# Layer 2 of batches 0 and 1 as seven quarter products, in a fused cross attention and maxout kernel

## The chip, the cores and the metric

The kernel runs on one core of one Trainium2 chip, alone. A core has five engines that run side by side and meet through semaphores: TensorE (PE; its weight loads are listed as PEld), VectorE (DVE), ScalarE (ACT), GpSimd (POOL) and SyncE (SP), which here issues nearly all DMAs. The metric is the device time of one execution in microseconds (us), the median of several runs; less is better.

## The reference

There are 8 batches, 8 heads, 512 tokens and 32 state rows of 64 columns per head. Each batch has a cross attention in both directions, and all of its 544 rows then go through a layer with two weight matrices of which the larger product is kept:

```python
scores = scale * np.matmul(x, state.transpose(0, 1, 3, 2))     # a = softmax(scores)
xread = np.matmul(a, state)
scores2 = scale * np.matmul(state, x.transpose(0, 1, 3, 2))    # a2 = softmax(scores2)
sread = np.matmul(a2, x)
x = np.concatenate([xread, sread], axis=2)                     # as rows of 8 * 64 = 512 columns
g = np.maximum(x @ w1, x @ w2)                                 # 512 -> 1024
out = g @ w_out                                                # 1024 -> 512
```

## The kernel before, in words

The larger of two products is written as relu(x (w1 - w2)) + x w2. So the kernel computes wd = w1 - w2 and wwo = w2 w_out once, and the output is relu(x wd) w_out + x wwo. For the token rows, x is A S (attention weights times state), so S is multiplied with wd and wwo first: for each batch that gives the small matrix `sw` (two groups of four heads, 1024 columns for wd and 512 for wwo, `sw_mm`, three pieces called 0, 1 and w). Layer 1 is then `l1_mm`: for each of 8 blocks f of 128 hidden columns two matmuls of `sw` with A^T (`at`), 512 columns wide, into one bank of PSUM; `relu` empties it into `r` (bf16). Layer 2 is r w_out plus A times the wwo part of `sw`; this last part is called the opening here.

Layer 2 comes in two forms. The plain one (`l2_mm`) computes for each of four chunks of 128 tokens eight matmuls with `r` and two with `at`, all 512 columns wide: 40 per batch. The other treats tokens, hidden columns and output columns each in halves, and so `r` and w_out each as 2 x 2 quarters: with sums of quarters made beforehand, seven products of quarters do for the eight of the plain form (`product`, eight matmuls of 256 columns each: four hidden blocks by two token chunks). The sums of w_out's quarters are `wt` (`w_sum` 0 to 3, once), those of r's quarters are `st` (`r_sum` 0 to 3, per batch). The products pile up in three banks called X, Y and Z: X takes products 1, 6, 7 and 4 one after the other, and between them its contents are copied to `part` (`keep`) or, with a part added, to a quarter of the output (`put`); Y takes 5 and 3, Z takes 2. `opened` adds the opening (four matmuls of 256 columns), for one quarter with the difference of two halves of `sw` (`difference`, on POOL). Before the change batches 0 and 1 use the plain form, batches 2 to 7 the other.

Where no loop says otherwise, the order is what is written. Up to the end of batch 1 the order of all engines comes from a table of tokens, ORDER: each token is a step with its batch, its part, its engine (>A is ACT, >V DVE, >P POOL) and its banks (@). It starts weights, batches 0 and 1, and the attention of batch 2. From batch 2 on a loop takes over: layer 1 of batch b, then its seven products, with scores, exponentials, `sw` and the transposes of batch b + 1 between them. A^T and X^T are made by transposing DMAs on SP's queue (`at_dma`, `xt_dma`), X^T from bf16 copies that POOL casts (`cast_b`); `cast_e` makes another copy for the state read (`sr_mm`, the attention's other direction). Every engine takes its instructions strictly in the order written, so one that waits holds up all behind it.

The state reads of batches 0 and 1 are picked out of a larger product: `srw_mm` computes more than is needed, `srw_ev` copies it to `srx`, and `sr_pick` takes four blocks per batch from it, on POOL. The ring of banks for short-lived results is `RELEASE`.

In the listings bank_63 is bank 0, bank_64 bank 1 and so on; r_105 is `r` of even batches, r_106 of odd ones; sw_102, sw_103 and sw_104 are `sw` of batches 0, 1 and 2; big_112 holds `wt`, big_114 `st`, big_115 `part` and `dif`, big_109 and big_111 the outputs of batches 0 and 1, big_117 x of batch 2, big_118 x of batch 3.

Of the kernel before, what the change touches and what calls it, by code (L numbers as in the profile page):

```python
# [8 lines left out]
F32 = mybir.dt.float32  # L9
# [33 lines left out]
mul.2.0>P l2.1.1.1@0 le.1.3>A sc.2.1@1 l2.1.1.2@0 ce.3.0>P exp.2.1>A l2.1.0.1@7 ce.3.1>P l2.0.2.3@2 red.2.1>V
l2.1.2.1@5 cb.3.0>P l2.0.3.0@3 le.1.2>V l2.0.0.3@6 mul.2.1>P l2.1.1.0@0 l2.0.0.2@6 l2.1.1.o@0 ce.3.3>P atd.2
l2.1.0.3@7 ce.3.2>P le.1.1>A l2.0.3.2@3 le.1.0>V l2.0.0.0@6 cb.3.1>P le.0.3>A sr.2@0 le.0.0>V sw.2.0@3,7 xtd.3
ldx.5.0 ldx.5.1
sw.2.w@5,1 sre.2>V swe.2.0.0>A sw.2.1@6,4 l2.0.2.0@2 swe.2.w.1>A swe.2.w.0>V l2.0.1.3@0 swe.2.1.1>A l2.0.2.1@2
swe.2.0.1>V l2.0.1.o@0 le.0.2>A l2.0.1.2@0 swe.2.1.0>A l2.0.1.0@0 srt.2@2 l2.0.1.1@0 srte.2>A le.0.1>V store.0
"""

LATE = 2

WHOLE = ()

RELEASE = [3, 1, 5, 4, 7, 6, 2, 0]


@with_exitstack
def kernel(
# [9 lines left out]
    nc = tc.nc  # L69
# [31 lines left out]
    def copy(eng, o, i):  # L101
        if eng == "A":
            nc.scalar.copy(o, i)  # L103
        elif eng == "V":
            nc.vector.tensor_copy(o, i)  # L105
        else:
            nc.gpsimd.tensor_copy(o, i)  # L107
# [168 lines left out]
    def red(b, hh):  # L276
        nc.vector.tensor_reduce(es_all[:, b, hh], e_view(e_s[b % 2], hh), axis=AXX, op=ALU.add)  # L277
        nc.vector.reciprocal(er_s[b % 2][:, hh], es_all[:, b, hh])  # L278
# [104 lines left out]
    def l2_open(b, c, p, start, stop, lo=0, hi=DM):  # L383
        for g in range(2):
            nc.tensor.matmul(p[:, lo:hi], at_s[b % 3][:, g, c, :], sw_s[b % 3][:, g, FF + lo:FF + hi],  # L385
                             start=(start and g == 0), stop=(stop and g == 1))

    def l2_f(b, c, p, fs, start, stop, lo=0, hi=DM):
        for j, f in enumerate(fs):
            nc.tensor.matmul(p[:, lo:hi], r_s[b % 2][:, f, c * 128:(c + 1) * 128], wo[:, f, lo:hi],  # L390
                             start=(start and j == 0), stop=(stop and j == len(fs) - 1))
# [16 lines left out]
    def rq(b, i, j):  # L408
        return r_s[b % 2][:, 4 * j:4 * j + 4, 256 * i:256 * i + 256]
# [57 lines left out]
    def store(b, c0=0, c1=NC, lo=0, hi=DM, eng=None):  # L467
        dst = out[b * L:b * L + S].rearrange("(p c) n -> p c n", c=NC)
        (eng or nc.sync).dma_start(out=dst[:, c0:c1, lo:hi], in_=ob(b)[:, c0:c1, lo:hi])
# [110 lines left out]
    def l2_mm(b, c, q, ring):  # L580
        p, first, last = acc(f"l2{b}{c}", ring)
        if q == "o":
            l2_open(b, c, p, first, last)
        else:
            l2_f(b, c, p, (2 * q, 2 * q + 1), first, last)

    def sw_range(b, z):
        if z == "w":
# [254 lines left out]
```

## Time and profile before

| | |
|---|---|
| median of 3 runs | 147.07 us (146.77 to 147.42) |
| the profiled execution | 147.19 us, of which the span of its instructions 145.4 us |
| granted TensorE clock, mean | 0.989 |
| TensorE busy | 136.4 us, 94% of the span |
| VectorE, ScalarE, GpSimd busy | 98.3, 82.1 and 67.9 us |
| HBM traffic | 15.20 MB read, 8.91 MB written |

A line of the groups gives the kernel's line, engine and operation, output and inputs, how often, the busy time with the mean of one, and the idle time before with what ended it. A line of the timeline gives start, length, engine, line, operation and count; a line of the chain of waits gives start, length, engine and line. "SPq" is SP's queue of DMA issues; the time that a transfer takes to land is listed apart.

### The profile page before, as it was taken

What the parts mean: (1) busy time and instruction counts of PE and PEld (TensorE: products, weight loads), DVE (VectorE), ACT (ScalarE), POOL (GpSimd) and SP (SyncE); (2) the same over time, 40 slices, a digit from 0 to 9 for tenths busy, and PEclk for the clock granted to TensorE, in tenths of its full rate; (3) what the DMA queues carried; (4) which work ended last, traced back from release to release, by engine and by line L of the source; (5) the groups of instructions that cost most, each with busy time, mean ns of one, the idle gap of its engine ahead of it and who ended that gap; (6) DMA issues with size and microseconds to landing.
All of it is one profiled execution on the core that took longest, in us unless ns stands there. A gap on an engine that the chain in (4) does not pass through costs nothing.

```text
span 145.4 us, 3491 instructions
## 1 busy us (share of the span) xinstructions
PE 136.4 (94%) x1376; PEld 89.0 (61%) x1388; DVE 98.3 (68%) x181; ACT 82.1 (56%) x157; POOL 67.9 (47%) x95
## 2 busy tenths in 40 slices
PE   6888999999999999999999999999999999999950
PEld 2566735444454446785778478757867784885840
DVE  3488969783324648997899789489948896941300
ACT  4457789898122675845781768268556817831110
POOL 4147320198979990498079509923930630000000
PEclk9999999999999999999999999999999999999995
DMA  3999999939991599999976991487316034202451
GB/s 126 331 364 394 384 387 385 327 58 174 243 359 59 97 251 393 369 136 275 384 123 138 347 285 33 72 288 149 67 42 252 7 72 185 113 0 72 155 181 38
DMA packets 36468, 29.50 MB, mean 203 GB/s; under 512 B 22624, under 2 KB 32352, under 8 KB 35552
## 3 DMA queue, kind: packets, MB, share of 16 engines
q1 hardware_dynamic: 36176, 29.10, 68.9%
q8 instruction: 12, 0.20, 0.6%
q10 hardware_dynamic: 272, 0.13, 0.3%
q14 instruction: 8, 0.07, 0.2%
HBM read 15.20 MB, written 8.91 MB: 166 GB/s over the span
## 4 chain that ended last, share of the span: by engine, by line
PE 83%; DMA 11%; ACT 1%; issue 1%; DVE 1%; SPq 0%; DVEq 0%
PE bank L427 26%; PE bank L376 19%; PE bank L390 9%; DMA big<-in_moe_w_out_dram 8%; PE bank L433 7%; PE bank L353 4%; DMA big<-in_x_dram 3%; PE bank L578 3%; PE bank L474 2%; PE bank L484 2%; PE bank L385 2%; PE bank L265 2%; PE bank L305 1%; PE bank L482 1%; ACT wo L103 1%
## 5 line engine op out<-in xcount | busy, mean ns | idle before, releaser
L371 DVE TENSOR_SCALAR r<-bank 128x512 bf16<-128x512 f32 x32 | 21.8, 691 | 13.0 <-PE bank L376 12.6
L281 POOL TENSOR_TENSOR a<-e,er 128x512 bf16<-128x512 bf16 x14 | 16.6, 1195 | 29.5 <-ACT e L273 22.5
L376 PE MATMUL bank<-at,sw 128*128 128x512 bf16 x122 | 29.4, 379 | 0.5 <-DVE sw L105 0.2
L103 ACT COPY big<-bank 128x512 f32<-128x512 f32 (+1 forms) x29 | 16.9, 587 | 17.5 <-PE bank L427 6.6
L103 ACT CAST sw<-bank 128x512 bf16<-128x512 f32 x35 | 19.5, 606 | 4.0 <-PE bank L353 4.0
L427 PEld LDWEIGHTS <-big 128*128 128x128 bf16 x192 | 17.9, 98 | 5.1 <-DVE er L278 2.1
L369 ACT ACTIVATE r<-bank 128x512 bf16<-128x512 f32 x32 | 18.5, 597 | 4.5 <-PE bank L376 4.2
L376 PEld LDWEIGHTS <-sw 128*128 128x128 bf16 x128 | 12.3, 98 | 14.1 <-ACT sw L103 0.5
L107 POOL CAST xe<-big 128x512 bf16<-128x512 f32 x27 | 17.7, 688 | 6.2 <-DMA big<-in_x_dram 6.2
L427 PE MATMUL bank<-big,big 128*128 128x256 bf16 x144 | 17.1, 273 | 0.0
L107 POOL CAST xb<-big 128x1024 bf16<-128x1024 f32 x12 | 12.2, 1040 | 7.2 <-DMA big<-in_x_dram 7.2
L390 PE MATMUL bank<-wo,r 128*128 128x512 bf16 x61 | 15.2, 379 | 0.3 <-issue 0.2
L427 PEld LDWEIGHTS <-r 128*128 128x128 bf16 x144 | 13.7, 98 | 2.6
L403 DVE TENSOR_TENSOR big<-bank,big 128x512 f32<-128x512 f32 (+1 forms) x19 | 12.3, 654 | 2.9 <-PE bank L433 2.9
L277 DVE TENSOR_REDUCE sums<-e 128x16 f32<-128x512 bf16 x16 | 10.6, 664 | 5.1 <-ACT e L273 5.0
L103 ACT COPY sread_t<-bank 128x128 bf16<-128x128 bf16 x8 | 3.3, 473 | 16.9 <-PE bank L337 13.7
L273 ACT ACTIVATE e<-bank 128x512 bf16<-128x512 f32 x16 | 9.0, 601 | 5.8 <-PE bank L265 5.7
L427 PE MATMUL bank<-wo,r 128*128 128x256 bf16 x96 | 12.3, 273 | 0.0
L433 PE MATMUL bank<-sw,at 128*128 128x256 bf16 x72 | 10.8, 273 | 0.0
L390 PEld LDWEIGHTS <-r 128*128 128x128 bf16 x64 | 5.9, 98 | 7.0 <-issue 0.5
L433 PEld LDWEIGHTS <-at 128*128 128x128 bf16 x96 | 9.4, 98 | 1.1
L403 DVE TENSOR_TENSOR big<-r 128x1024 bf16<-128x1024 bf16 x12 | 9.2, 767 | 0.6
(86 smaller groups left out, 195.9 us busy)
## 6 DMA issues: line engine op xcount, KB each, us to landing
big<-in_x_dram SPq DMA_DIRECT2D x16, 512.0 KB, 5.5
out_dram<-big SPq DMA_DIRECT2D x7, 1024.0 KB, 5.4
big<-in_moe_w_dram SPq DMA_DIRECT2D x8, 512.0 KB, 11.7
big<-in_moe_w_out_dram SPq DMA_DIRECT2D x4, 512.0 KB, 11.7
out_dram<-big SPq DMA_DIRECT2D x4, 256.0 KB, 3.5
sf<-in_state_dram SPq DMA_DIRECT2D x1, 384.0 KB, 10.4
out_dram<-w2m SPq DMA_DIRECT2D x1, 256.0 KB, 2.5
out_dram<-w2m SPq DMA_DIRECT2D x2, 128.0 KB, 3.1
```

What stands on the lines that cost most here:

```text
L103: nc.scalar.copy(o, i)
L107: nc.gpsimd.tensor_copy(o, i)
L273: nc.scalar.activation(out=e_view(e_s[b % 2], hh).rearrange("p (g c) i n -> p g c (i n)", g=2), in_=p.rearrange("p (c g m) -> p g c m", c= ...
L277: nc.vector.tensor_reduce(es_all[:, b, hh], e_view(e_s[b % 2], hh), axis=AXX, op=ALU.add)
L281: (nc.gpsimd if eng == "P" else nc.vector).tensor_mul(e_view(a_s[b % 2], hh), e_view(e_s[b % 2], hh), er_s[b % 2][:, hh].unsqueeze(3).to_b ...
L369: nc.scalar.activation(out=o, in_=p, func=ACTF.Relu)
L371: nc.vector.tensor_scalar(o, p, scalar1=0.0, scalar2=None, op0=ALU.max)
L376: nc.tensor.matmul(p, sw_s[b % 3][:, g, f * 128:(f + 1) * 128], at_s[b % 3][:, g].rearrange("p c t -> p (c t)"), start=(g == 0), stop=(g = ...
L390: nc.tensor.matmul(p[:, lo:hi], r_s[b % 2][:, f, c * 128:(c + 1) * 128], wo[:, f, lo:hi], start=(start and j == 0), stop=(stop and j == le ...
L403: (nc.gpsimd if eng == "P" else nc.vector).tensor_tensor(o, i0, i1, op=op)
L427: nc.tensor.matmul(pv[c], lhs[:, f, 128 * c:128 * c + 128], rhs[:, f, :], start=first and f == 0 and (c == 0 or pv.split), stop=False, ski ...
L433: nc.tensor.matmul(pv[c], at_s[b % 3][:, g, 2 * i + c, :], rhs[:, g, :], start=False, stop=False, skip_group_check=True)
```

## The change

Batches 0 and 1 use the seven products too. The tokens of the plain form go from the end of the table, and tokens for sums, products, copies and additions come in (p1 to p7, o3, o4, o7 and p2o for the openings, k0 to k2 for `keep`, v00 to v11 for `put`, rs for `r_sum`, dif). Besides:

- `srx` lies in the input buffer of batch 1 and not in the buffer of batch 2's small matrix, and the picks stand on POOL ahead of batch 2's casts.
- Four casts of batch 2 (ce.2) move from POOL to ACT; the weight sums 2 and 3 move from POOL to DVE.
- The store of batch 0 is issued ahead of X^T of batch 3; that of batch 1 in the loop, behind A^T of batch 3.
- `RELEASE` names the banks in another order.
- The last copy of the state rows' output is one on ACT and not two halves on DVE and ACT; in the branch for out-of-range sums, which isn't taken, a store is split.

```diff
-swe.0.w.0>V l2.1.3.2@4 ce.2.1>P l1.0.3@3 l1.0.1@1 re.1.2>A ce.2.2>P l1.1.0@6 re.0.3>A re.0.1>V l2.0.2.2@2 l1.0.6@7
...
+p1.0@1 k0.0>A p1.1@4 rs.0.2>V wt.2>V v00.0 p6.0 rs.0.3>V k0.1>A k1.0>A p5.0@7 wt.3>V v00.1 rs.1.0>V k2.0>A
+sc.2.0@6 exp.2.0>A sc.2.1@0 exp.2.1>A sw.2.0@5,3 red.2.0>V mul.2.0>P red.2.1>V swe.2.0.0>A swe.2.0.1>A ce.2.0>A ce.2.1>A ce.2.2>A ce.2.3>A
+p7.0 o7.0 v11.0 rs.1.1>V mul.2.1>P p3.0 o3.0 rs.1.2>V atd.2 sw.2.w@6,2 swe.2.w.0>A v01.0 swe.2.w.1>A
+p4.0 o4.0 rs.1.3>V ce.3.0>P ce.3.1>P cb.3.0>P ce.3.2>P ce.3.3>P cb.3.1>P v10.0>A store.0 xtd.3 dif.1>P
+sr.2@0 p6.1 k1.1>A sw.2.1@5,3 sre.2>V swe.2.1.0>A swe.2.1.1>V p5.1@7 k2.1>A
+p7.1 o7.1 v11.1 p3.1 o3.1 v01.1 srt.2@0 srte.2>A p4.1 o4.1 v10.1>A ldx.5.0 ldx.5.1
...
-RELEASE = [3, 1, 5, 4, 7, 6, 2, 0]
+RELEASE = [1, 6, 2, 5, 3, 0, 4, 7]
...
-    srx = sw_s[2].rearrange("p g w -> p (g w)")[:, 0:2080].bitcast(F32).rearrange("p (b g k z) -> p b g k z", b=2, g=2, k=4)
+    srx = big[7][:, 0:1040].rearrange("p (b g k z) -> p b g k z", b=2, g=2, k=4)
...
+    def fresh(kind, b, lhs, rhs, at):
+        pairs[kind, b] = Pair(at)
+        product(pairs[kind, b], lhs, rhs, True)
...
+        p1=lambda b, at: fresh("X", b, rq(b, 0, 0), wq(0, 0), at), p2=lambda b, at: fresh("Z", b, rq(b, 0, 1), wq(1, 0), at),
+        p5=lambda b, at: fresh("Y", b, st[:, 0], wt[:, 0], at), p6=lambda b: product(pairs["X", b], st[:, 1], wt[:, 1]),
+        p7=lambda b: product(pairs["X", b], st[:, 2], wt[:, 2]), p3=lambda b: product(pairs["Y", b], st[:, 3], wq(1, 1)),
+        p4=lambda b: product(pairs["X", b], rq(b, 1, 1), wt[:, 3]),
...
+        k0=lambda b, e: keep(0, pairs["X", b], e), k1=lambda b, e: keep(1, pairs["X", b], e),
+        k2=lambda b, e: keep(2, pairs["Y", b], e), v00=lambda b: put(b, 0, 0, pairs["Z", b], 0),
+        v11=lambda b: put(b, 1, 1, pairs["X", b], 2), v01=lambda b: put(b, 0, 1, pairs["Y", b], 1),
+        v10=lambda b, e: put(b, 1, 0, pairs["X", b], None, e),
...
-    store(1)
...
-    w_sum(3, "P")
...
+        if b == 2:
+            store(1)
...
-    m2(1, "VA", "r", 256, 512)
+    m2(1, "A", "r", 256, 512)
```

Three places show what stands where now. On DVE, from the last evacuation of layer 1 of the first two batches (L371 before, L370 now) through the two reductions of batch 2, before:

```order
L371 TENSOR_SCALAR r_106<-bank_64 128x512
L277 TENSOR_REDUCE sums_79<-e_91 128x16
L278 RECIPROCAL er_95<-sums_79 128x16
L277 TENSOR_REDUCE sums_79<-e_91 128x16
L278 RECIPROCAL er_95<-sums_79 128x16
L105 COPY big_111<-bank_68 128x512
L105 COPY big_111<-bank_70 128x512
```

and now, from the third sum of batch 0's r on:

```order
L402 TENSOR_TENSOR big_114<-r_105 128x1024
L402 TENSOR_TENSOR big_112<-wo_77 128x1024
L402 TENSOR_TENSOR big_109<-bank_66,big_115 128x2x256
L402 TENSOR_TENSOR big_114<-r_105,big_114 128x1024
L402 TENSOR_TENSOR big_112<-wo_77,big_112 128x1024
L402 TENSOR_TENSOR big_111<-bank_65,big_115 128x2x256
L402 TENSOR_TENSOR big_114<-r_106 128x1024
L276 TENSOR_REDUCE sums_79<-e_91 128x16
L277 RECIPROCAL er_95<-sums_79 128x16
L276 TENSOR_REDUCE sums_79<-e_91 128x16
L277 RECIPROCAL er_95<-sums_79 128x16
L402 TENSOR_TENSOR big_109<-bank_64,big_115 128x2x256
```

Before, nothing stood between the evacuations and the reductions, and plain copies of output chunks followed. Now sums, weight sums and additions stand ahead of the reductions, and the last row, which empties X of batch 0 (bank_64) into quarter (1,1), stands behind them.

On POOL, from the casts of batch 2 (big_117) to the attention weights of batch 2 (a_93), before:

```order
L107 CAST xb_89<-big_117 128x4x4x64
L107 CAST xe_86<-big_117 128x2x4x64 x3
L107 COPY wz_73<-sw_104 32x130 x8
L403 TENSOR_TENSOR big_112<-wo_77 128x1024 x2
L403 TENSOR_TENSOR big_112<-wo_77,big_112 128x1024
L281 TENSOR_TENSOR a_93<-e_91,er_95 128x8x64
```

and now:

```order
L402 TENSOR_TENSOR big_112<-wo_77 128x1024
L106 CAST xb_89<-big_117 128x4x4x64
L402 TENSOR_TENSOR big_112<-wo_77,big_112 128x1024
L402 TENSOR_TENSOR big_115<-sw_102 128x512
L280 TENSOR_TENSOR a_93<-e_91,er_95 128x8x64 x2
```

The eight picks (L107 COPY) stand ahead of these rows now; a weight sum has come between the two casts that X^T of batch 2 is made from, and the four casts to xe_86 are gone to ACT.

On SP, from A^T of batch 2 (at_101) to A^T of batch 3 (at_99) and what follows it, before:

```order
L286 DMA_TRANSPOSE at_101<-a_93 128x8x128
L243 DMA_TRANSPOSE xt_88<-xb_90 128x16x128
L168 DMA big_113<-in_x_dram 128x4x256 x2
L469 DMA out_dram<-big_109 128x2048
L469 DMA out_dram<-big_111 128x2048
L243 DMA_TRANSPOSE xt_87<-xb_89 128x16x128
L286 DMA_TRANSPOSE at_99<-a_94 128x8x128
L168 DMA big_117<-in_x_dram 128x4x256 x2
```

and now:

```order
L285 DMA_TRANSPOSE at_101<-a_93 128x8x128
L468 DMA out_dram<-big_109 128x2048
L242 DMA_TRANSPOSE xt_88<-xb_90 128x16x128
L167 DMA big_113<-in_x_dram 128x4x256 x2
L242 DMA_TRANSPOSE xt_87<-xb_89 128x16x128
L285 DMA_TRANSPOSE at_99<-a_94 128x8x128
L468 DMA out_dram<-big_111 128x2048
L167 DMA big_117<-in_x_dram 128x4x256 x2
```

The store of batch 0 (big_109) stands ahead of X^T of batch 3 (xt_88); that of batch 1 (big_111) has moved past X^T of batch 4 and A^T of batch 3, to just ahead of the loads of batch 6.

More of the change, by code (lines that the diff above doesn't have):

```diff
@@ L33 @@
 ww.1.3@7 sub.2.1>V ate.1.0>A ww.0.3@1 swre.1.1>A sw.1.1@0,6 sw.0.1@5,3 swe.1.1.0>A swe.1.1.1>V ww.2.3@4 swe.0.1.0>A
-swe.0.1.1>V l1.1.5@6 cw2.1>P l1.1.7@0 cw2.0>A re.1.5>V l1.0.7@3 w2.1@5 re.1.7>V re.0.7>A w2.0@6 w2e.1>V cwo.0>A
+swe.0.1.1>V l1.1.5@6 cw2.1>P srp.0>P srp.1>P l1.1.7@0 cw2.0>A re.1.5>V l1.0.7@3 w2.1@5 re.1.7>V re.0.7>A w2.0@6 w2e.1>V cwo.0>A
 l1.0.5@3 l1.1.6@0 w2e.0>V l1.1.4@5 cwo.1>A ww.2.0@4 re.0.5>V ww.1.0@7 re.1.4>A ww.2.1@4 sub.0.0>V ww.1.1@7 re.1.6>A
 sub.0.1>V ww.3.0@2 wwe.2>A ww.0.1@1 sub.1.1>V ww.3.1@2 wwe.1>A ww.0.0@1 sub.1.0>V wwe.3>A l1.0.4@7 wwe.0>A cb.2.0>P
-sw.0.0@2,4 re.0.4>V sw.1.0@0,5 swe.0.0.1>A sw.0.w@1,3 swe.1.0.1>V sw.1.w@7,6 ce.2.0>P swe.1.0.0>A l2.1.3.3@4
@@ L43 @@
[L43 to L48, printed above, removed]
+sw.0.0@2,4 re.0.4>V wt.0>P sw.1.0@0,5 swe.0.0.0>A swe.0.0.1>V sw.0.w@1,3 sw.1.w@7,6 cb.2.1>P swe.1.0.0>A swe.1.0.1>V xtd.2 wt.1>P
@@ new lines @@
+p2.1@2 l1.0.6@4 swe.0.w.0>A re.0.6>V l1.0.3@0 l1.0.2@5 swe.0.w.1>A re.0.3>V swe.1.w.0>V mS.1>A
+l1.0.1@4 l1.0.0@1 p2.0@3 swe.1.w.1>V mS.0>A Sd dif.0>P re.0.2>V re.0.1>A re.0.0>A p2o.0
+l1.1.0@7 l1.1.1@6 l1.1.2@0 l1.1.3@5 re.1.0>V re.1.1>A re.1.2>A rs.0.0>V rs.0.1>V re.1.3>A
+p2o.1 ldx.4.1 ldx.3.0 ldx.4.0 ldx.3.1
+p1.0@1 k0.0>A p1.1@4 rs.0.2>V wt.2>V v00.0 p6.0 rs.0.3>V k0.1>A k1.0>A p5.0@7 wt.3>V v00.1 rs.1.0>V k2.0>A
+sc.2.0@6 exp.2.0>A sc.2.1@0 exp.2.1>A sw.2.0@5,3 red.2.0>V mul.2.0>P red.2.1>V swe.2.0.0>A swe.2.0.1>A ce.2.0>A ce.2.1>A ce.2.2>A ce.2.3>A
@@ L563 @@
         left[f"ww{i}"] = 4
-    for b in range(2):
-        for c in range(NC):
-            left[f"l2{b}{c}"] = 5
     def acc(key, ring):
@@ L578, in ww_mm @@
             nc.tensor.matmul(p, w2t[:, f, i, :], wo[:, f, :], start=(first and f % 2 == 0), stop=(last and f % 2 == 1))
[L580 to L585, printed above, removed]
+    pairs = {}
+    def fresh(kind, b, lhs, rhs, at):
+        pairs[kind, b] = Pair(at)
+        product(pairs[kind, b], lhs, rhs, True)
     def sw_range(b, z):
@@ L601 @@
         idle=idle, fill=lambda k, r: idle(1, r, 512 if k >= 100 else 256, k >= 200), cS=s_cast, mS=lambda z, e: s_mask(z, LATE, B, e), Sd=lambda: s_dma(LATE, B), ce=cast_e, cb=cast_b, xtd=xt_dma,
-        atd=at_dma, red=lambda b, h, e: red(b, h), mul=mul, cw2=w2_cast, sub=w_sub, cwo=wo_cast, ww=ww_mm, l2=l2_mm,
-        wwe=lambda i, e: copy(e, wwo[:, i, :], open_[f"ww{i}"]), le=lambda b, c, e: l2_out(b, c, open_[f"l2{b}{c}"], e),
-        wt=w_sum,
+        atd=at_dma, red=lambda b, h, e: red(b, h), mul=mul, cw2=w2_cast, sub=w_sub, cwo=wo_cast, ww=ww_mm,
+        wwe=lambda i, e: copy(e, wwo[:, i, :], open_[f"ww{i}"]),
+        wt=w_sum, rs=r_sum, dif=difference,
+        p1=lambda b, at: fresh("X", b, rq(b, 0, 0), wq(0, 0), at), p2=lambda b, at: fresh("Z", b, rq(b, 0, 1), wq(1, 0), at),
+        p5=lambda b, at: fresh("Y", b, st[:, 0], wt[:, 0], at), p6=lambda b: product(pairs["X", b], st[:, 1], wt[:, 1]),
+        p7=lambda b: product(pairs["X", b], st[:, 2], wt[:, 2]), p3=lambda b: product(pairs["Y", b], st[:, 3], wq(1, 1)),
+        p4=lambda b: product(pairs["X", b], rq(b, 1, 1), wt[:, 3]),
+        p2o=lambda b: opened(b, pairs["Z", b], 0, so_half(b, 0)), o7=lambda b: opened(b, pairs["X", b], 1, so_half(b, 1)),
+        o3=lambda b: opened(b, pairs["Y", b], 0, so_half(b, 1)), o4=lambda b: opened(b, pairs["X", b], 1, dif[:, b % 2]),
+        k0=lambda b, e: keep(0, pairs["X", b], e), k1=lambda b, e: keep(1, pairs["X", b], e),
+        k2=lambda b, e: keep(2, pairs["Y", b], e), v00=lambda b: put(b, 0, 0, pairs["Z", b], 0),
+        v11=lambda b: put(b, 1, 1, pairs["X", b], 2), v01=lambda b: put(b, 0, 1, pairs["Y", b], 1),
+        v10=lambda b, e: put(b, 1, 0, pairs["X", b], None, e),
         Se=lambda lo, hi, j, e: s_ev(done[f"S.{lo}.{hi}"], lo, hi, j, e), store=store,
@@ L811 @@
             m2(t, "V")
-            m_store(t, nc.gpsimd)
+            for k in range(2):
+                m_store(t, nc.gpsimd, 256 * k, 256 * k + 256)
 _INS = ['x', 'state', 'moe_w1', 'moe_w2', 'moe_w_out']
```

4 lines of the change are left out of this document (removed).

## The prediction, on record before the changed kernel ran

> **What bounds the kernel now.** I read the page's busy shares first, then the chain of waits in order of time, then the busy time by stage.
>
> ```profile
> span 145.4 us, 3491 instructions
> PE 136.4 (94%) x1376; PEld 89.0 (61%) x1388; DVE 98.3 (68%) x181; ACT 82.1 (56%) x157; POOL 67.9 (47%) x95
> ...
> 29.95 0.41 PE bank L353 x8
> 43.88 3.45 PE bank L390 x16
> 52.95 0.06 PE bank L337
> 53.44 3.45 PE bank L376 x16
> 56.89 0.87 PE bank L427 x8
> 57.76 0.47 PE bank L265 x16
> 59.10 0.44 PE bank L433 x4
> 59.54 0.77 PE bank L353 x24
> 63.52 0.36 PE bank L305 x32
> ...
> 30.36:53.44 23.08, 22.82 (x169) 10.71 (x173) 10.28 (x20) 11.70 (x21) 21.60 (x27) 1.00 0.71 171
> ```
>
> The first rows are the page's; the chain's give start, length and work; the stage rows give the stretch, its length, and the busy time of PE, PEld, DVE, ACT and POOL, then the granted clock. From 29 us to the tail the chain is TensorE alone. The stage that the change rewrites runs from 30.36 (the last small matrix of batches 0 and 1, 29.95 + 0.41) to 53.44 (layer 1 of batch 2): TensorE is busy 22.82 of 23.08 us at full clock, DVE only 10.28. So TensorE work taken out there is time won, as long as DVE and ACT, which get more work, don't become what TensorE waits for; and what is won at 53.44 lasts only if the inputs of the later batches, which TensorE uses up without gaps, come earlier too.
>
> **TensorE's work.** Before, layer 2 of batches 0 and 1 is 80 matmuls of 512 columns; sixteen take 3.45 us (0.216 each): 17.25 us. Now it is 14 products of eight matmuls of 256 columns at 0.87 and 8 openings of four at 0.44: 15.70. The saving is 1.55 us, the most that this stage can give beside its 0.26 us of gaps.
>
> The Trainium skill has a rule that speaks against this (TensorE: Matmul & The Clock Gate, Back-to-back issue gap): it gives a sustained 131 ns for 512 columns and 81 for 128, which taken at its word makes 144 narrow matmuls (at least 11.7 us, an estimate from that page) dearer than 80 wide ones (10.5): 1.2 us lost. The trace disagrees: 216 ns for 512 columns and 109 for 256, just what the same section calls the isolated gap.
>
> **What DVE and ACT must now do in that stage.** Rows for the durations (start, length, engine):
>
> ```profile
> 29.58 2.05 ACT L103 CAST sw<-bank 128x512 bf16<-128x512 f32 x4 [0.16 <-PE bank L353]
> 29.89 2.48 DVE L105 CAST sw<-bank 128x512 bf16<-128x512 f32 x4
> 31.55 0.94 ACT L223 ACTIVATE sb<-sf,mask 128x768 bf16<-128x768 f32 x1
> 53.27 3.62 PE L376 MATMUL bank<-at,sw 128*128 128x512 bf16 x16
> 53.90 0.60 ACT L369 ACTIVATE r<-bank 128x512 bf16<-128x512 f32 x1 [0.41 <-PE bank L376]
> 57.72 0.69 DVE L403 TENSOR_TENSOR big<-r 128x1024 bf16<-128x1024 bf16 x1
> 58.45 0.69 DVE L403 TENSOR_TENSOR big<-big,r 128x1024 bf16<-128x1024 bf16 x1
> 59.06 0.68 DVE L277 TENSOR_REDUCE sums<-e 128x16 f32<-128x512 bf16 x1
> 60.17 2.51 POOL L281 TENSOR_TENSOR a<-e,er 128x512 bf16<-128x512 bf16 x2 [5.65 <-DVE er L278]
> 60.77 1.00 DVE L403 TENSOR_TENSOR big<-r 128x1024 bf16<-128x1024 bf16 x1
> 63.70 0.68 DVE L403 TENSOR_TENSOR big<-bank,big 128x512 f32<-128x512 f32 x1
> L103 ACT CAST xe<-big 128x512 bf16<-128x512 f32 x3 | 1.9, 618 | 3.5 <-DMA big<-in_x_dram 3.4
> ```
>
> A sum over 1024 columns takes DVE 0.69 us alone (one start to the next 0.73 as at 57.72, where it uses the one before; else I take 0.61 to 0.65, near the four casts in 2.48) and 1.00 beside POOL's products (60.17). An addition from a bank takes 0.68; two reductions with reciprocals run from 59.06 to 60.77, 1.71. An evacuation starts 0.20 us after its two matmuls (53.27 + 0.43, then 53.90). I now walk the new order from 30.36.
>
> TensorE: product 2 of batch 1 (0.87), five first-layer matmul pairs of batch 0 (0.43 each, with 0.1 of waiting for a bank), product 2 of batch 0 and its opening (1.31) end at 34.8. Batch 1's last four pairs follow; DVE evacuates the first of them from 35.4 to 36.05 and then has an unbroken queue: sums 0, 1, 2 of batch 0 (0.73 + 0.73 + 0.61), weight sum 2 (0.65), an addition (0.68), sum 3 (0.65), weight sum 3 (0.69), an addition (0.68), sum 0 of batch 1 (0.65), two reductions of batch 2 (1.71), and only then the addition that empties X of batch 0 into quarter (1,1), 0.68: done at **44.5**.
>
> TensorE meanwhile: the four pairs end at 36.53, the opening at 36.97, product 1 of both batches at 38.71, products 6 and 5 of batch 0 (after 0.05 for ACT's copy of X) at 40.5, scores 0.47, the small matrix 0.26 (a third of L353's 0.77), product 7 and opening 1.31, product 3 and opening 1.31, small matrix 0.26: **44.1**. Product 4 adds on to X, so it waits for DVE until 44.6: 0.5 us lost. Behind it on TensorE stands all else, state read of batch 2 first.
>
> ACT: four casts, two masked copies of the state (0.94 each) and five evacuations of layer 1 end at 37.6, just ahead of its first copy of X; the copies of banks (0.59) and two exponentials end at 42.5; two evacuations (0.52 each) and the four casts of batch 2 that POOL had (0.62 each) end at 46.0. Product 4 ends at 45.9 with its opening; the state read needs those casts: 0.2 lost. Then state read 0.36, product 6 of batch 1 0.87, small matrix 0.26, product 5 0.87: 48.46. ACT's copy of X of batch 1, behind two evacuations and quarter (1,0) of batch 0, ends at 48.3, so no wait. Three products with openings (3.93) and the transpose 0.06 bring layer 1 of batch 2 to **52.45** instead of 53.44: **-0.99 us**, that is, 1.55 of work and most of 0.26 of gaps less some 0.8 of new waits. Bounds: none of these waits, and layer 1 starts at 51.65 (-1.8); or DVE's seven sums before 44.5 all at 1.00, 2.2 us later (+1.2). I take my walk, because POOL has nothing between its difference for batch 0 and the products of batch 2:
>
> ```profile
> 28.67 1.04 POOL L107 CAST xb<-big 128x1024 bf16<-128x1024 f32 x1 [7.19 <-DMA big<-in_x_dram]
> 32.89 2.62 POOL L107 COPY wz<-sw 32x130 f32<-32x130 f32 x8
> 35.59 4.20 POOL L403 TENSOR_TENSOR big<-wo 128x1024 bf16<-128x1024 bf16 x2
> 43.95 1.17 POOL L107 CAST xe<-big 128x512 bf16<-128x512 f32 x2
> 31.30 2.06 SPq L243 DMA_TRANSPOSE xt<-xb  x1
> 49.23 1.80 SPq L243 DMA_TRANSPOSE xt<-xb  x1
> 54.23 0.84 SPq L469 DMA_DIRECT2D out_dram<-big  x2
> 55.17 7.74 SPq L243 DMA_TRANSPOSE xt<-xb  x1
> 63.02 1.86 SPq L286 DMA_TRANSPOSE at<-a  x1
> DMA to landing us min/median/max: 4.3/4.3/4.3
> DMA to landing us min/median/max: 10.6/10.6/10.6
> DMA to landing us min/median/max: 5.9/6.1/6.3
> sbd<-sb SPq DMA_TRANSPOSE x1, 3.7
> ```
>
> **The moved pieces.** The eight picks (2.62 us) go to POOL's idle 7.19 us before 28.67: free, and what they read is batch 1's dead input buffer. POOL from 28.67: cast 1.04, weight sum 2.1, cast 1.04, weight sum 2.1, difference some 1.2: 36.2. So X^T of batch 2 is issued at 32.9, not 31.3, and lands 4.3 later at 37.2 (the first landing row is that of 31.30 and of 49.23, the second that of 55.17, the third that of the two at 82 and 95 us). The state's transpose goes 2.06 after it and takes 3.7: 38.7. Scores read both at 40.5: hidden. At 43.0 POOL multiplies, and then has batch 3's casts without a break: 45.1 + four at 0.59 + two at 1.04, 49.6 to 50. X^T of batch 3 is thus issued about 0.6 late, and behind batch 0's store, which now goes out at 47.8 instead of 54.23. Alone it landed in 4.3 us; behind two stores and two loads (55.17) in 10.6. Here one store has a start of 2 us: I take 54 to 55 (the later ones, straight behind one store, land in 5.9 and 6.3). Its reader starts at 52.45 + 3.45 + 0.87 = 56.8: hidden with about 2 us. Batch 1's store moves behind the A^T issue of 63.02 and in front of two loads that are cast some 14 us later: nothing on the path.
>
> **The tail.**
>
> ```profile
> 139.00 0.37 ACT L103 COPY w2m<-bank 128x256 f32<-128x256 f32 x1 [0.88 <-PE bank L484]
> 140.31 0.29 DVE L105 COPY w2m<-bank 128x128 f32<-128x128 f32 x1 [3.24 <-PE bank L484]
> 140.63 0.27 ACT L103 COPY w2m<-bank 128x128 f32<-128x128 f32 x1 [1.26 <-DVE w2m L105]
> ```
>
> The two half copies ran one after the other to 140.90; one of 0.37 from 140.31 ends at 140.68: -0.22 us, ahead of the last store.
>
> Sum: 147.19 (the profiled execution: 145.4 of span and 1.8 around it, which I leave) - 0.99 - 0.22 = 145.98. The median of the runs is 0.12 below that execution: **145.9 us**.
>
> **Rivals.**
> - *All of the work is saved* (DVE's queue is done by 44.1 and ACT's casts too): 0.7 less, 145.2. For it: DVE's starts lie as close as 0.60; against it: both waits stand on full queues.
> - *DVE is the new bound.* Its 10.28 busy us grow by ten sums and six additions less the copies out, to some 18.5 of 21.5. If its seven sums before X's addition run at 1.00 as at 60.77, product 4 waits until 46.8 and all behind it is 2.2 us late: 148.2, slower. It decides from 1.2 us of extra lateness on. Against it: POOL is idle there.
> - *X^T of batch 3 is late.* Landing in 10.6 us puts the scores at 60.4, 3.6 late: 149.6. Against it: half the traffic ahead.
> - *Narrow matmuls cost more than half of wide ones.* A matmul of 256 columns that takes 0.120 instead of 0.109 eats all 1.55: 147.5 with my waits and the tail. Against it: the 0.87 rows, in every batch from 2 on. The skill's sustained figures above would end here, on the slow side.
>
> **How the numbers follow.** My walk 0.50 (own range 145.4 to 146.6), all saved 0.15, DVE the bound in whole or part 0.24, X^T late 0.08, narrow matmuls or anything else that voids the change 0.03. About 0.5% (0.74 us) is what a measurement of this kernel can tell from no change, so faster means below 146.33. Of the walk 0.42 lies below that, all of the second, and 0.04 of the third (a lateness under 0.4): 0.61. Slower, above 147.8: 0.08 of the third, 0.05 of the fourth: 0.13. The rest is 0.26. The range 145.0 to 147.4 leaves out only the full DVE case and the late X^T.
>
> **What would show it.** In the trace of the changed kernel: 144 matmuls of 256 columns between 30 and 53 us at 0.87 for eight; layer 1 of batch 2 at 52.45 (51.7 if all is saved, 54.6 if DVE binds); one TensorE wait of about 0.5 us ahead of product 4 of batch 0, released by a DVE addition; DVE without gaps from 36 to 48; X^T of batch 3 landed by 55; one 0.37 us copy at the end. I am wrong if TensorE waits over 1.5 us in that stage, or if a wait in the pass of batch 2 takes back what was won.

## The result, and the profile after

The changed kernel takes **145.74 us** (median of 9 runs, 145.60 to 146.72), the kernel before beside it 147.30 us (9 runs, 146.77 to 147.61). The ratio is 0.9908, with a 95% interval of 0.9887 to 0.9929: 1.35 us less, or 1.56 by the medians. The profiled execution took 145.66 us, its span 143.9.

The page of the changed kernel, its first rows and busy shares:

```profile
span 143.9 us, 3646 instructions
PE 136.0 (95%) x1441; PEld 95.2 (66%) x1452; DVE 106.8 (74%) x191; ACT 86.3 (60%) x166; POOL 65.3 (45%) x91
```

TensorE is busy 0.4 us less than before and not 1.55; VectorE has 8.5 us more. (A second profiled execution of the changed kernel has 135.3 us for TensorE, so this row by itself decides little.) The busy time by stretch (stretch, length, busy time of PE, PEld, DVE, ACT and POOL with their instructions, granted clock, DMA share, GB/s) shows the rewritten stage and the two passes behind it:

```profile
30.30:52.64 22.34, 22.22 (x235) 16.78 (x237) 19.29 (x32) 15.35 (x29) 15.33 (x15) 1.00 0.81 203
52.64:66.08 13.44, 13.39 (x162) 9.51 (x162) 11.74 (x22) 8.00 (x16) 9.03 (x11) 1.00 0.80 205
66.08:79.58 13.50, 13.43 (x162) 9.48 (x162) 11.93 (x23) 8.44 (x18) 8.28 (x10) 1.00 1.08 266
```

The stage took 23.08 us before and takes 22.34: 0.74 us of the 1.55 are won, and TensorE has nearly no gaps (0.12 us). The chain of waits of the changed kernel (start, length, engine and line) shows what became of the rest:

```profile
30.30 0.98 PE bank L426 x8
...
38.80 1.91 PE bank L426 x16
...
41.17 0.34 PE bank L352 x8
41.51 0.98 PE bank L426 x8
...
42.93 0.87 PE bank L426 x8
...
44.24 0.34 PE bank L352 x8
44.58 0.98 PE bank L426 x8
...
46.35 0.98 PE bank L426 x8
47.34 0.34 PE bank L352 x8
```

A product (L426, eight matmuls) takes 0.87 us, but 0.98 when it stands right behind a run of small tiles (the small matrix L352, the state read L304). And a third of the small matrix takes 0.34 by itself, where all three thirds in one place take 0.77, 0.26 each. The weight loads, some matmuls and two rows of ScalarE and VectorE of the changed kernel's timeline (start, length, line, what is loaded, and the idle time before with what ended it) show where the 0.11 comes from:

```profile
37.83 0.68 DVE L402 TENSOR_TENSOR big<-wo 128x1024 bf16<-128x1024 bf16 x1
37.95 0.59 ACT L102 COPY big<-bank 128x512 f32<-128x512 f32 x1 [0.65 <-PE bank L426]
38.77 1.66 PEld L426 LDWEIGHTS <-big 128*128 128x128 bf16 x16 [0.32 <-DVE big L402]
...
41.10 0.11 PEld L352 LDWEIGHTS <-sbd 64*32 64x32 bf16 x8
41.44 0.77 PEld L426 LDWEIGHTS <-big 128*128 128x128 bf16 x8 [0.23 <-issue]
...
42.66 0.86 PEld L426 LDWEIGHTS <-big 128*128 128x128 bf16 x8
42.76 1.04 PE L426 MATMUL bank<-wo,big 128*128 128x256 bf16 x8
...
44.51 1.05 PE L426 MATMUL bank<-big,r 128*128 128x256 bf16 x8
44.51 0.77 PEld L426 LDWEIGHTS <-r 128*128 128x128 bf16 x8 [0.23 <-issue]
```

Between products of full tiles, the first weights are loaded 0.10 us ahead of the first matmul (42.66 and 42.76). Behind the 64x32 tiles the load waits, and starts with the matmuls (44.51 both). The Trainium skill (TensorE: Matmul & The Clock Gate, "Step-by-step: what each phase is for") says that TensorE takes a weight load ahead of running matmuls where their row groups don't conflict, or into the spare weight buffer; these rows agree as far as the 0.10 goes, and why a load is not taken ahead behind small tiles no run here shows.

By work alone (14 products at 0.87, 8 openings at 0.44, 9 pairs of layer 1 at 0.43, scores 0.47, three thirds at 0.257, state read 0.36, transpose 0.06) the stage is some 21.25 us. The other 1.1 are: five products behind small tiles, 0.11 each; 0.22 for products 6 and 5 of batch 0 at 38.80, whose first weights wait (row 38.77 above), the one wait for another engine in the stage; three lone thirds, 0.25 together; small gaps in layer 1, 0.08. The profile puts that wait down to VectorE, of which a sum of quarters of w_out (row 37.83) ended at 38.51. But that sum is for product 7, and the two that product 6 reads had ended by 34.85 and 37.31. What product 6 must wait for is ScalarE's copy of X, onto which it adds: row 37.95, done at 38.54. The two ends lie 0.03 apart, so the trace does not separate them; the kernel's text speaks for ScalarE. Before, the same stage lost only 0.27 in such ways. It had the three thirds in one place, as its chain shows:

```profile
49.42 0.83 PE bank L353 x24
50.25 0.16 issue
```

SP's queue in the changed kernel's timeline (start, length of the issue, line, kind): L468 are stores, L242 X^T, L167 loads of X, L285 A^T.

```profile
50.65 2.99 SPq L242 DMA_TRANSPOSE xt<-xb  x1
...
63.92 0.52 SPq L468 DMA_DIRECT2D out_dram<-big  x1
...
67.71 7.64 SPq L242 DMA_TRANSPOSE xt<-xb  x1
75.44 2.04 SPq L285 DMA_TRANSPOSE at<-a  x1
```

The issue of X^T of batch 5 (67.71) stands on the queue for 7.64 us, with batch 1's store, two loads and batch 2's store ahead of it. Next in the queue is A^T of batch 4, which lands 4.1 us after 75.44, at 79.54; its reader starts at 79.58. So there is a second bound beside TensorE, and it touches it here.

The passes behind take what they took before to 0.03 us, except that of batch 4, which starts at this landing: 13.43 us instead of 13.30. TensorE ends at 139.60 (before: 140.29), the last copy at 139.99 (before: 140.90), and from there to the span's end it is 3.9 us (before: 4.5).

### The profile page after: what moved, and what is told of

The parts are those of the page before. It is cut to its first block, busy times and chain, and to the rows that moved or that the text cites. A ratio compares the mean times of both kernels' runs of the same rounds, so it can differ in the third digit from the quotient of the medians.

```text
span 143.9 us, 3646 instructions
## 1 busy us (share of the span) xinstructions
PE 136.0 (95%) x1441; PEld 95.2 (66%) x1452; DVE 106.8 (74%) x191; ACT 86.3 (60%) x166; POOL 65.3 (45%) x91
## 4 chain that ended last, share of the span: by engine, by line
PE 86%; DMA 6%; SPq 2%; ACT 1%; issue 1%; DVE 0%; DVEq 0%
PE bank L426 36%; PE bank L375 19%; PE bank L432 10%; DMA big<-in_moe_w_dram 6%; PE bank L352 5%; PE bank L574 4%; PE bank L473 2%; PE bank L483 2%; PE bank L264 2%; PE bank L304 2%; PE bank L516 1%; SPq L167 1%; PE bank L481 1%; PE bank L291 1%; ACT wb L102 1%
## 5 line engine op out<-in xcount | busy, mean ns | idle before, releaser
L370 DVE TENSOR_SCALAR r<-bank 128x512 bf16<-128x512 f32 x32 | 21.9, 690 | 11.9 <-PE bank L375 10.8
L102 ACT COPY big<-bank 128x512 f32<-128x512 f32 (+2 forms) x37 | 20.8, 566 | 16.1 <-PE bank L426 8.4
L426 PEld LDWEIGHTS <-big 128*128 128x128 bf16 x256 | 23.9, 98 | 6.5 <-DVE er L277 2.1
L426 PE MATMUL bank<-big,big 128*128 128x256 bf16 x192 | 23.1, 273 | 0.1
L426 PEld LDWEIGHTS <-r 128*128 128x128 bf16 x192 | 18.2, 98 | 3.7 <-issue 0.5
L402 DVE TENSOR_TENSOR big<-bank,big 128x512 f32<-128x512 f32 (+1 forms) x25 | 16.4, 660 | 3.8 <-PE bank L432 3.7
L426 PE MATMUL bank<-wo,r 128*128 128x256 bf16 x128 | 16.3, 273 | 0.0
L432 PE MATMUL bank<-sw,at 128*128 128x256 bf16 x96 | 14.4, 273 | 0.0
L432 PEld LDWEIGHTS <-at 128*128 128x128 bf16 x128 | 12.5, 98 | 1.7
L402 DVE TENSOR_TENSOR big<-r 128x1024 bf16<-128x1024 bf16 x16 | 12.6, 790 | 0.6
L402 POOL TENSOR_TENSOR big<-sw 128x512 bf16<-128x512 bf16 x8 | 9.2, 1154 | 0.9 <-POOL a L280 0.9
L426 PE MATMUL bank<-wo,big 128*128 128x256 bf16 x64 | 8.3, 273 | 0.0
```

The lines of the kernel that those rows point to most:

```text
L370: nc.vector.tensor_scalar(o, p, scalar1=0.0, scalar2=None, op0=ALU.max)
L402: (nc.gpsimd if eng == "P" else nc.vector).tensor_tensor(o, i0, i1, op=op)
L426: nc.tensor.matmul(pv[c], lhs[:, f, 128 * c:128 * c + 128], rhs[:, f, :], start=first and f == 0 and (c == 0 or pv.split), stop=False, ski ...
L432: nc.tensor.matmul(pv[c], at_s[b % 3][:, g, 2 * i + c, :], rhs[:, g, :], start=False, stop=False, skip_group_check=True)
```

## The experiments

Two theories. **A:** what was lost of the 1.55 us goes at the changes between small and full tiles; VectorE and ScalarE are not what TensorE waits for; and part of the gain rests on the stores having been moved out of the way of the A^T transposes. **B (the prediction's walk):** VectorE's queue costs 0.5 us ahead of product 4 of batch 0, and the stores' places are worth nothing.

**Changes between small and full tiles, doubled.** In the loop the three thirds of the small matrix are put in three places, third 1 behind product 6 and the third w behind product 5; nothing else differs from the changed kernel.

```diff
-        pg = [sw_mm(n, 512 * z, 512 * z + 512, BY if z == 0 else "r") for z in range(3)]
+        pg = [sw_mm(n, 0, 512, BY)]
...
+        pg.append(sw_mm(n, 512, 1024))
...
+        pg.append(sw_mm(n, 1024, 1536))
```

> The changed kernel, but in the loop over batches 2 to 6 the three pieces of the next batch's small matrix no longer stand in one block on TensorE: pieces 1 and w go behind products 6 and 5, so each stands alone between products, as batch 2's pieces do in the changed stage. Same work. Theory 1 (each change between small tiles and full ones costs TensorE about 0.2 us in all: 0.08 at a lone piece, 0.34 against 0.26, and 0.11 at the eight matmuls behind it, 0.98 against 0.87): two more such places in each of 5 passes, 1.9 us more than the changed kernel, 147.6. Theory 2 (those extra times are waits for DVE and ACT, as the prediction had it): nothing, 145.7 to 145.9.

Measured: 148.51 us (148.28 to 148.84), ratio to before 1.0094 (1.0062 to 1.0127), 2.77 us above the changed kernel. The chain of waits of this kernel:

```profile
58.81 0.34 PE bank L352 x8
59.15 0.98 PE bank L426 x8
...
61.79 0.98 PE bank L426 x8
...
64.70 2.09 DVE sr L312 x2
...
67.13 3.45 PE bank L375 x16
```

The same three products and three thirds take 3.96 us where the changed kernel takes 3.54 (0.77 + 2.77): 0.42 for two more changes, with the very figures 0.34 and 0.98. Five passes of this would make 2.1 us. Pass by pass the kernel is 0.98 and 0.97 us longer in the first two, and 0.21 to 0.41 in the other three. In the first two TensorE also waits ahead of L336, 0.55 and 0.60, for the last rows of a state read on VectorE (64.70 above): an addition ahead of them starts later (63.31 instead of 62.90), and they take 2.1 us instead of 1.5. That a change costs, and how much where it stands, is shown; the total came out above the forecast because of these two waits.

**VectorE's slack.** One sum in front of the addition in question is done three times (a repeated step, with the same result).

```diff
-... wt.3>V v00.1 rs.1.0>V k2.0>A
+... wt.3>V v00.1 rs.1.0>V rs.1.0>V rs.1.0>V k2.0>A
```

> The changed kernel with sum 0 of batch 1 computed three times over instead of once, so DVE's queue ahead of the addition that empties X of batch 0 is two sums (1.2 us) longer. In the changed kernel's trace that addition ends at 44.21, lands at about 44.4, and product 4 starts at 44.58: some 0.15 us of slack. If DVE is next to binding there, product 4 and all behind it come 1.05 us later: 146.8. If DVE has room (its queue catches up, the waits are elsewhere): 145.7 to 145.9.

Measured: 146.63 us (146.37 to 146.92), ratio 0.9956 (0.9936 to 0.9977), 0.89 above the changed kernel. The chain of waits of this kernel, at product 4 of batch 0:

```profile
44.87 0.64 DVE big L402
45.51 0.04 issue
45.55 1.03 PE bank L426 x8
```

The two further sums make the addition end at 45.51 instead of 44.21, and product 4 start at 45.55 instead of 44.58. This execution is 0.12 us late already ahead of them, so the addition is 1.18 later and product 4 0.85: VectorE has 0.3 us of slack there in the changed kernel. Rows of VectorE and ScalarE in the changed kernel's timeline say the same:

```profile
43.58 0.63 DVE L402 TENSOR_TENSOR big<-bank,big 128x512 f32<-128x512 f32 x1
44.13 1.46 DVE L402 TENSOR_TENSOR big<-big,r 128x1024 bf16<-128x1024 bf16 x1
43.13 2.22 ACT L102 CAST xe<-big 128x512 bf16<-128x512 f32 x4
```

The addition is done at 44.21, and product 4 could start at 44.58 only because TensorE itself was late. VectorE is the next bound, not the bound: theory B's wait ahead of product 4 does not exist.

**Small pieces side by side.** In the table, third 1, the third w and the state read move together, and product 5 of batch 1 goes ahead of product 4 of batch 0.

```diff
-... atd.2 sw.2.w@6,2 swe.2.w.0>A v01.0 swe.2.w.1>A
+... atd.2 p5.1@2 k2.1>A v01.0
...
-sr.2@0 p6.1 k1.1>A sw.2.1@5,3 sre.2>V swe.2.1.0>A swe.2.1.1>V p5.1@7 k2.1>A
+p6.1 k1.1>A sr.2@0 sw.2.1@5,3 sw.2.w@6,7 sre.2>V swe.2.1.0>A swe.2.1.1>V swe.2.w.0>A swe.2.w.1>A
```

> The changed kernel with fewer changes of tile: pieces 1 and w of batch 2's small matrix and its state read stand in one block on TensorE behind product 6 of batch 1, and product 5 of batch 1 (in bank 2) takes the place ahead of product 4 of batch 0. Same work. Theory 1 (changes of tile cost): two changes fewer, about 0.35 us less than the changed kernel, 145.4, and layer 1 of batch 2 at 52.3 instead of 52.64. Theory 2 (waits for DVE and ACT): product 4 no longer has room for its DVE addition or keeps it, the same 145.7.

Measured: 145.42 us (145.17 to 145.75), ratio 0.9885 (0.9855 to 0.9914). Its chain of waits:

```profile
30.40 0.98 PE bank L426 x8
...
47.44 0.36 PE bank L304 x32
47.80 0.56 PE bank L352 x16
48.35 0.98 PE bank L426 x8
...
52.52 3.45 PE bank L375 x16
```

The stage is 22.12 us instead of 22.34, 0.22 less. That agrees with theory A's figure for two changes taken away (0.2 to 0.4). The medians (0.3 apart) say the same, but intervals as wide as these don't tell the two kernels apart.

**The stores back at their old places**, in the changed kernel.

```diff
-... cb.3.1>P v10.0>A store.0 xtd.3 dif.1>P
+... cb.3.1>P v10.0>A xtd.3 dif.1>P
-... v10.1>A ldx.5.0 ldx.5.1
+... v10.1>A ldx.5.0 ldx.5.1 store.0 store.1
-        if b == 2:
-            store(1)
```

> The changed kernel with the stores of batches 0 and 1 where they stood before (both behind the loads of batch 5, ahead of X^T of batch 4). If the stores' places cost or bring nothing on TensorE's path: 145.7 to 145.9. If A^T of batch 3 behind a full queue would hold up layer 1 of batch 3, as it did to within 0.1 us before: 0.3 to 1 us more, 146.0 to 146.7.

Measured: 148.70 us (147.87 to 149.86), ratio 1.0119 (1.0078 to 1.0159): 3.0 us above the changed kernel, and slower than before. The rows of SP, GpSimd and TensorE in the timeline of this kernel:

```profile
55.40 8.82 SPq L242 DMA_TRANSPOSE xt<-xb  x1
59.41 2.50 POOL L280 TENSOR_TENSOR a<-e,er 128x512 bf16<-128x512 bf16 x2 [4.43 <-DVE er L277]
64.32 2.28 SPq L285 DMA_TRANSPOSE at<-a  x1
68.47 1.89 PE L375 MATMUL bank<-at,sw 128*128 128x512 bf16 x7 [2.36 <-DMA at<-a]
```

GpSimd has A of batch 3 ready at 61.91. Its transpose is not issued before X^T of batch 4, ahead of it in the queue, is through at 64.22: layer 1 of batch 3 starts at 68.47 instead of 66.08. In the kernel before the same jam (7.74 us) ended at 62.91, and TensorE came to that point 0.8 us later; the jam was there, but it was just covered (A^T landed at 66.72, and layer 1 of batch 3 began at 66.87). The products use up the cover. Neither expectation was of this size. The profiled execution (147.87 us) is the fastest of the six, and this wait is all that it lost; what the others, up to 149.86, lost besides has no trace.

**Batch 0's store alone back**, batch 1's where the change puts it.

```diff
-... cb.3.1>P v10.0>A store.0 xtd.3 dif.1>P
+... cb.3.1>P v10.0>A xtd.3 dif.1>P
-... v10.1>A ldx.5.0 ldx.5.1
+... v10.1>A ldx.5.0 ldx.5.1 store.0
```

> One edit on the changed kernel: batch 0's store goes back behind the loads of batch 5, batch 1's stays behind A^T of batch 3. Theory (3 us come only with both stores ahead of X^T of batch 4): X^T of batch 4 stands some 6.5 us on the queue instead of 4.13, until 61.7, A^T of batch 3 is issued at 62 as before, layer 1 of batch 3 at 66.1: 145.8. Rival (one store ahead of that X^T is enough): A^T of batch 3 issued at 63 or later, layer 1 of batch 3 at 67 or later, 146.7 to 148.

Measured: 146.03 us (145.61 to 147.29), ratio 0.9928 (0.9901 to 0.9955). SP's queue in the timeline of this kernel:

```profile
54.90 7.02 SPq L242 DMA_TRANSPOSE xt<-xb  x1
62.03 1.25 SPq L285 DMA_TRANSPOSE at<-a  x1
```

With one store ahead X^T of batch 4 stands 7.02 us, until 61.92, when GpSimd is just done (61.78): next to nothing is lost at this batch in the profiled execution. Runs up to 147.29 suggest that little margin is left. By the medians the one store costs 0.3 us (against 145.71 on the same chip, below) and both cost 3.0; batch 1's alone at its old place was not tried.

**Parts of the change without the products**, on the kernel before: the picks early, `srx` in batch 1's input buffer, batch 1's store behind A^T of batch 3, and one copy at the end. Layer 2 stays plain, and batch 0's store, the casts of batch 2 and `RELEASE` stay as they were.

```diff
+... cw2.1>P srp.0>P srp.1>P l1.1.7@0 ...
...
-    srx = sw_s[2].rearrange("p g w -> p (g w)")[:, 0:2080].bitcast(F32).rearrange("p (b g k z) -> p b g k z", b=2, g=2, k=4)
+    srx = big[7][:, 0:1040].rearrange("p (b g k z) -> p b g k z", b=2, g=2, k=4)
...
-    store(1)
...
+        if b == 2:
+            store(1)
-    m2(1, "VA", "r", 256, 512)
+    m2(1, "A", "r", 256, 512)
```

> The kernel before with all of the change that can be had without the products: the picks ahead of batch 2's casts with their source in batch 1's input buffer, batch 1's store behind A^T of batch 3, one copy at the tail. Layer 2 of batches 0 and 1 stays plain. If the products carry the gain: 0.2 less than before, 147.1. If the moved pieces carry half of it: 146.5.

Measured: 148.13 us (147.88 to 148.37), ratio 1.0059 (1.0033 to 1.0084): these edits together, without the products, make the kernel slower by 0.9 us. The timeline of SP and TensorE there:

```profile
68.60 8.56 SPq L243 DMA_TRANSPOSE xt<-xb  x1
77.26 1.26 SPq L286 DMA_TRANSPOSE at<-a  x1
81.79 1.46 PE L376 MATMUL bank<-at,sw 128*128 128x512 bf16 x6 [1.32 <-DMA at<-a]
```

The jam has moved on by one batch, to X^T of batch 5, with the same neighbours as in the changed kernel. It stood 8.56 us here and 7.64 there; with 0.9 us less, some 0.4 of the wait of 1.32 would be left (an estimate). Why it is longer here stays open.

**Batch 1's store where the queue is empty**, behind A^T of batch 5 (`if b == 4`), in three kernels: the changed one, the one with the small pieces grouped, and the kernel before, where this is the only edit (there `store(1)` stood behind the table and goes from it).

```diff
-        if b == 2:
+        if b == 4:
             store(1)
```

> One edit on the changed kernel: batch 1's store goes behind A^T of batch 5 (pass of batch 4, where no loads of X stand in the queue) instead of behind A^T of batch 4's predecessor, batch 3. Theory (what stands on SP's queue ahead of an X^T holds up the A^T behind it): the issue of X^T of batch 5 takes about 5 us instead of 7.64, A^T of batch 4 is issued at about 75.4 as soon as GpSimd is done, takes 1.2 instead of 2.04 and lands near 78.7 instead of 79.54, layer 1 of batch 4 begins at 79.4 instead of 79.58: 145.6, and fewer runs near 146.7. Rival (the queue costs nothing as the kernel stands): 145.75, the same start of batch 4. Third way, the jam only moves on to A^T of batch 6: 146 to 147.

> The kernel with the small pieces of the state grouped, and batch 1's store behind A^T of batch 5. Both terms adding up: 145.42 less 0.16 (the wait for A^T of batch 4 there) = 145.25. If the start of batch 4 is not what the store costs: 145.4.

> The kernel before with one edit: batch 1's store behind A^T of batch 5. Theory (before loses nothing to SP's queue, since its A^T of batch 3 lands at 66.72 for a reader at 66.75, and the gain is the work of the products): 147.2 to 147.3, X^T of batch 4 stands 6.5 to 7 us instead of 7.74, layer 1 of batch 3 no earlier than 0.05 us. Rival (the place of batch 1's store was part of the gain by itself): 146.9 or less.

> The changed kernel itself beside the three others on one chip: 145.75. If the second copy at the end costs 0.2 us, the kernel without that edit (146.42 on another chip) was mostly chip and spread, and this one reads 146.0 to 146.2; if it costs 0.7, this one reads 145.75.

Measured, the first three rows side by side on one chip:

| kernel | us | ratio to before |
|---|---|---|
| changed, again | 145.71 (145.49 to 146.30) | 0.9887 (0.9865 to 0.9910) |
| changed, store 1 late | 145.35 (145.26 to 145.76) | 0.9869 (0.9847 to 0.9890) |
| grouped, store 1 late | 145.29 (145.10 to 145.99) | 0.9851 (0.9831 to 0.9871) |
| before, store 1 late | 147.02 (146.79 to 147.59) | 0.9987 (0.9968 to 1.0006) |

SP's queue in the changed kernel with that store late:

```profile
67.69 4.88 SPq L242 DMA_TRANSPOSE xt<-xb  x1
75.38 1.23 SPq L285 DMA_TRANSPOSE at<-a  x1
```

X^T of batch 5 stands 4.88 instead of 7.64 us, and A^T of batch 4 takes 1.23 to issue and 3.1 to land instead of 2.04 and 4.1. A^T is not issued earlier, since GpSimd has it ready only at 75.35; what is won is its landing, at 78.5 instead of 79.54. For TensorE, which is there at 79.4, this is worth 0.1 to 0.2. The other traces agree: from the start of L336's matmuls to layer 1 of batch 4 it is 0.15 to 0.39 us in the six profiled executions with seven products and batch 1's store behind A^T of batch 3 (the kernel with its small pieces split, where VectorE holds L336 back, left out), and 0.12 in both that have it late. The medians go down by 0.36 and the runs lie closer together, which is the forecast's direction; the intervals overlap. Grouping adds nothing that can be told on top of it. In the kernel before, the same edit changes nothing that can be measured, as theory A had it: its queue had cover.

**The tail.** One copy at the end on the kernel before, and the two halves put back into the changed kernel:

```diff
-    m2(1, "VA", "r", 256, 512)
+    m2(1, "A", "r", 256, 512)
```

> The kernel before with the one copy at the tail instead of two halves, and nothing else. By the copies' rows: 0.2 less than before, 147.1. If the earlier landing of the last store (2.5 us after issue instead of 3.1) comes with that copy as well: 0.8 less, 146.5.

> The changed kernel with the two half copies back at the tail. By the copies' rows: 0.2 more than the changed kernel, 145.95. If the last store's earlier landing comes with the one copy: 0.8 more, 146.5.

Measured: alone 147.13 us against 147.29, ratio 0.9989 (0.9968 to 1.0010), 0.16 less, not told from nothing; with the halves back 146.42 us (145.66 to 147.12), ratio 0.9934 (0.9912 to 0.9956), 0.7 above the changed kernel as run on another chip. The profiled execution with the halves shows them one after the other to 140.44, 0.61 behind TensorE's end at 139.83, against 0.39 with one copy: 0.2. That execution (146.01 us) is only 0.35 above the profiled one of the changed kernel, and its chain of waits holds the rest:

```profile
75.56 4.17 DMA at<-a
```

A^T of batch 4 lands at 79.73 there and TensorE waits for it 0.13 longer than in the changed kernel (0.39 against 0.26 from L336 to layer 1); that wait has nothing to do with the copies. The changed kernel gave 145.74 and 145.71 in two series, so it repeats well; why the median with the halves lies another 0.4 above its profiled execution stays open.

## Why the prediction was right, and where it wasn't

The time (145.9 against 145.74) and the sign were right. The working had TensorE's work right and the waits in its way wrong: the sign that it named, a wait of 0.5 us ahead of product 4 ended by an addition of VectorE, is not in the trace.

- **TensorE's work, -1.55.** Right as far as the matmuls themselves go: 8 openings at 0.44, and products at 0.87 wherever full tiles stand before them; five of the 14 took 0.98 for what stood ahead. The rival of dear narrow matmuls is out.
- **The new waits, +0.8, of which DVE 0.5 and ACT 0.2.** The size was near (layer 1 of batch 2 at 52.64, forecast 52.45, and 22.34 us of stage for 22.09), the cause wrong. The step that failed is the one that has TensorE ready at 44.1: it costed each third of the small matrix at 0.26, "a third of L353's 0.77", though the diff puts the thirds in three places, and each product at 0.87 whatever stood before it. It measured 0.34 and 0.98, which is 0.27 of the 0.48 by which TensorE came later to product 4, at 44.58; another 0.17 is the wait at products 6 and 5, 0.22 where the walk had 0.05. VectorE's addition was done at 44.21, 0.3 earlier than walked, and ScalarE's casts at 45.35 instead of 46.0. So the two waits of the walk, 0.7, were not there, and changes between tiles, at 0.8 for the stage, were there unforeseen; that the sizes are alike is luck. Row 49.42 against row 59.54 of before (0.83 and 0.16 of issue, against 0.77) hinted that such a change has a price; I read past it.
- **DVE the bound.** Against it, rightly: it didn't decide. But the slack is only 0.3 us, and sums beside GpSimd's work took up to 1.46 us (44.13 above), more than the 1.00 of the rival; they stood behind the addition in question, so that cost nothing there.
- **X^T of batch 3.** Right: issued at 50.65 (forecast 49.6 to 50), landed 4.4 later at 55.05, its reader at 56.97.
- **"Batch 1's store: nothing on the path".** As a cost, near enough: 0.1 to 0.4. As a reading it was the gravest gap. I looked for a late X^T, and only for batch 3's. What an X^T issue holds up is the A^T behind it in the queue, which is due in some 4 us, while X^T itself had 5 to spare. Row 55.17 of before (7.74 us on the queue) and row 63.02 (A^T issued right at its end) stood in my own fence. The rival as I wrote it would have named the right mechanism if I had asked who stands behind that row; then the stores' moves would have appeared as what they are, the condition of the gain: products without them 148.70, batch 1's store moved (with the picks and the copy) without products 148.13, all together 145.74.
- **The tail, -0.22.** Right: 0.61 from TensorE's end to the copy's end became 0.39.
- **The sum.** -0.99 and -0.22 were forecast. The profiled executions show -0.80 at layer 1 of batch 2, of which 0.69 is left at TensorE's end (the 0.11 goes at A^T of batch 4), and -0.22 for the copy: 0.91, not 1.21. That the spans differ by 1.5 comes from the last stores, where before had 4.5 us and the changed kernel 3.9. So part of the agreement is luck.

With batch 1's store out of the way in both kernels the products and the other edits give 147.02 - 145.35 = 1.67 us (on two chips; the ratios, 0.9987 and 0.9869, give as much).

## What to carry to other kernels

When a stage gets shorter, go through every queue of the stage behind it and ask what was late there but covered: an issue that stands for 8 us on an in-order queue is a bound for whatever is next in that queue, not only for its own reader. Price a piece of work at its place, with what stands before and behind it: here a third of a group that was moved out alone cost 0.34 us and not 0.26, and small tiles made the product behind them 0.11 dearer. And try the parts of a change apart: here the products without the stores' moves, and some of the moves without the products, each made the kernel slower.

## What was unexpected of the hardware

- A change from small tiles (64x32, 128x32) to full ones cost 0.11 us at the product behind, and a lone run of eight small matmuls 0.08 more than its share of a longer one; two further changes in a pass cost 0.42.
- The issue of a transposing DMA is not over when it is handed on. On SP's queue that of X^T stood 1.8 to 3.1 us where no load or store had been issued in the 3 us before, 3.9 to 4.3 right behind two loads, 4.2 to 7.4 behind one store, and 6.0 to 8.8 behind two stores and two loads; nothing behind it in that queue started in the meantime. The Trainium skill (DMA: Bandwidth & Descriptors, "Queues, rings and completion order") has each DMA engine take up what stands in its ring in order, which agrees; how long the issue itself is held, these runs alone show.
- From the end of the last copy to the end of the span it is 4.0 to 4.5 us in the four kernels with plain layer 2, and 3.7 to 3.9 in the ten with seven products, though the last stores are the same. The two groups differ in a second thing, the split store in the branch that isn't taken, and no run takes the two apart; the cause is open.
